# A spectral filter and a gated MLP on one core: early root table, one-tensor small sums, a moved zero fill and another load order of the filter

## The chip, the cores and the metric

The kernel runs on one core of a Trainium2 chip. The metric is the device time of the core in microseconds (us); lower is better.

The engines, as the profile names them: PE is TensorE (matmuls), PEld its weight loads, DVE is VectorE, ACT is ScalarE, POOL is GpSimd, SP is SyncE, which here only issues DMA transfers ("SPq" in a line is its queue).

## The reference, cut to what matters

```python
x = A_x                                               # 1 x 2048 x 576, bf16
X = rfft2(layernorm(x)); X = X * (w_r + 1j * w_i)     # complex filter, 2048 x 289
h  = x + irfft2(X)
h2 = h + (gelu(LN(h) @ w_gate) * (LN(h) @ w_up)) @ w_down   # 576 -> 4608 -> 576
```

The transform is done as matmuls with tables. The MLP is about 430 us of dense matmuls. Before it come three stages that this study is about:

- **Stage A**, layer norm and the first transform. x comes in 16 tiles (0 to 15). For each tile, VectorE or ScalarE takes the sums, then a root on ScalarE, a reciprocal on VectorE, a scaling of the table ATB into ATS, and matmuls.
- **Stage F**, the filter, 16 groups. Each group has a matmul step D, a step B, a product T with the filter (VectorE), sums Z and ZR (VectorE), a step V, and for every four groups a step R. ScalarE moves the results of D (to CUS), B (to YS) and V out of the accumulators, "evictions"; the 16 small pieces of R (to VR) go out on VectorE or ScalarE.
- **The inverse stage**, which needs all of F, and ends with the first gate/up matmul of the MLP.

## The kernel before: the parts that matter

Each engine runs its own queue in the order in which the program lists the operations; the letters in two long strings are that order (cut here).

```python
SEQ1 = "k14 B0 S3 B1 v0 q0 B2 c0 n0 Q3 v1 x0D q1 S5 Q5 c1 x1P M0 ..."   # stage A
SEQF = "D0 D1 D2 B0 B1 T0 T1 D3 D4 B2 Z1 Z0 B3 T2 T3 D5 ..."            # stage F
RENG = [[dve,dve,act,dve],[dve,dve,dve,act],[act,dve,dve,dve],[dve,act,dve],[dve]]  # who evicts R

# SP issues, in this order: x tiles and tables, then 36 small transfers of the filter
for f in w_loads(1, 0, SP) + w_loads(0, 0, SP) + w_loads(0, 1, SP) + w_loads(1, 1, SP): f()
#        imaginary half 1    real half 1          real half 2          imaginary half 2
P.op(POOL, memset(VR, 0.0), w=["Vz"])                 # zero fill, at the start

# small sums of a tile whose statistics ScalarE took: two SBUF tensors each
P.op(DVE, scalar_tensor_tensor(TM, SA0, 1/(D*D), SA0, mult, mult))
P.op(DVE, scalar_tensor_tensor(MV, SA1, 1/D, TM, mult, subtract))

for i in range(16):                                   # "flips": minus the imaginary plane
    P.op(POOL, tensor_scalar(WS[:, g, 0], WS[:, g, 2], -1.0, ...),
         r=[imaginary half of g, ("ATS", 15)], w=[("Wn", i)])
# T(i):  TP = YS * WS     waits for YS(i), both planes of its half, and flip i
# VR evictions wait for the zero fill ("Vz")
```

Of the kernel before, what the change touches and what calls it, by code (L numbers as in the profile page):

```python
# [6 lines left out]
ACTF = mybir.ActivationFunctionType  # L7
ALU = mybir.AluOpType

S, D, K2 = 2048, 576, 289  # L10
KW = 288
HK = 144
NZ = 5
ABASE = 1
FF = 4608
NT = 16
# [3 lines left out]
EPS = 1e-5  # L20
NPRE = 8
GROUPS = ((0, 2), (2, 4), (4, 7), (7, 10), (10, 13), (13, 16))
SEQ1 = """k14 B0 S3 B1 v0 q0 B2 c0 n0 Q3 v1 x0D q1 S5 Q5 c1 x1P M0 B4 E1A B6 v2 E2A E3D n1 B7 q2 E4A n2 c2 B11 B8 E0A Q9 S9 x2P k104 M1 E5A E9A v3 B10 E6A B12 q3 c3 v4 E7A E8A x3D n3 S14 k202 M2 E11A n4 E14D E10A q4 Q14 E12A c4 B13 B15 v5 E13A M3 x4P E15A E16A q5 E18A E17D M4 E19A c5 x5D E20A E21D E22D n5 M5 E23A E25A E26A E27A E24D E28D E29A""".split()
ACT_TILES = tuple(int(w[1:]) for w in SEQ1 if w[0] == "Q")
SEQF = """D0 D1 D2 B0 B1 T0 T1 D3 D4 B2 Z1 Z0 B3 T2 T3 D5 D6 V1 Z2 B4 Z3 D7 V0 B5 T4 Z4 T5 D8 B6 R0 Z5 B7 D9 V3 T6 T7 B8 D10 Z6 B9 T8 V2 V4 D11 Z7 R1 Z8 B10 D12 T9 T10 V5 Z9 Z10 B11 V8 D13 B12 T11 V6 V7 Z11 D14 T12 R2 B13 Z12 D15 B14 T13 V11 Z13 B15 T14 V9 V12 Z14 V10 T15b T15a V14 V13 Z15b Z15a R4 V15 R3""".split()
RENG = [['dve', 'dve', 'act', 'dve'], ['dve', 'dve', 'dve', 'act'], ['act', 'dve', 'dve', 'dve'], ['dve', 'act', 'dve'], ['dve']]
QR = ((0, 2), (2, 4), (4, NPRE), (NPRE, 16))
SEQ = """I0 I1 N0 I2 s0 N1 I3 N2 m0 s1 I4 r0 q0 s2 N3 c0 m1 s3 n1 n0 r1 I5 q1 N4 I6 A1 c1 n3 A0 n2 N5 I7 D2 z3 N6 N7""".split()

# [277 lines left out]
def _build(nc, A_x, A_w_r, A_w_i, B_w_gate, B_w_up, B_w_down, out):  # L307
    P = Prog(nc)
    T = build_tables()
    dram = {n: nc.inline_tensor(_np_bf16(T[n]), name="c_" + n.lower()) for n in T}  # L310
    PE, DVE, ACT, SP, POOL = "pe", "dve", "act", "sp", "pool"
# [16 lines left out]
    VR = sb.alloc("VR", [128, NT, 2, NG, 8], BF16)  # L328
# [18 lines left out]
    MV1 = sb.alloc("MV1", [128, NT, 2], F32)  # L347
    SA = sb.alloc("SA", [128, 2, NT], F32)
    RS1 = sb.alloc("RS1", [128, NT], F32)
    SB2 = sb.alloc("SB2", [128, 2, NT], F32)  # L350
    TM = sb.alloc("TM", [128, 2, NT], F32)
    RS2 = sb.alloc("RS2", [128, NT], F32)
    EPT = sb.alloc("EPT", [128, 1], F32)
# [29 lines left out]
    TP = sb.alloc("TP", [128, 2, 2, 2, KW], BF16)  # L383
    ZS = sb.alloc("ZS", [128, NZ, 2, 256], BF16)
    ZR = sb.alloc("ZR", [128, 2, 2, 128], BF16)
# [14 lines left out]
        return PS[:, b * 512:(b + n) * 512].rearrange("p (a c) -> p a c", a=n)[:, :, 0:w]  # L400


    P.op(POOL, lambda g: g.memset(ZD[:, :], 0.0), w=["ZD"])
    P.op(POOL, lambda g: g.memset(EPT[:, :], EPS), w=["EPT"])
    xv = A_x[0].rearrange("(p c) d -> p c d", c=NT)
    ov = out[0].rearrange("(p c) d -> p c d", c=NT)
    tabs = dram["ATAB"].rearrange("p (c k) -> p c k", c=NT)
# [19 lines left out]
    def w_loads(pl, hf, eng):  # L427
        g0, g1 = ((1, 9), (9, 16))[hf]
        src = (A_w_r, A_w_i)[pl]
        o = []  # L430
        for jj in range(4):
            o.append((WS[jj:64:4, g0:g1, 1 + pl, :], 1 + (16 * jj + g0) * K2, [[128 * K2, 16], [K2, g1 - g0], [1, K2 - 1]], jj))
            o.append((WS[64 + jj:128:4, g0:g1, 1 + pl, :], 1 + (64 + 16 * jj + 16 - g0) * K2, [[128 * K2, 16], [-K2, g1 - g0], [1, K2 - 1]], 4 + jj))
        if hf:
            for p0 in range(2):
                o.append((WS[64 * p0:64 * p0 + 64, 0, 1 + pl, :], 1 + 64 * p0 * K2, [[128 * K2, 16], [16 * K2, 4], [1, K2 - 1]], 8 + p0))
        return [lambda d=d, off=off, ap=ap, h=h: P.dma(eng, d, bass.AP(src.tensor, off, ap), f"w{pl}{hf}", w=[("W", hf, pl, h)]) for d, off, ap, h in o]

    for f in w_loads(1, 0, SP) + w_loads(0, 0, SP) + w_loads(0, 1, SP) + w_loads(1, 1, SP):
        f()  # L440
    GORD = list(range(1, NG)) + [0]
    wkeys = [[("W", hf, pl, h) for pl in range(2) for h in range(8 + 2 * hf)] for hf in range(2)]
# [4 lines left out]
    P.dma(SP, IDT[:, :], dram["EYE"][:, :], "eye", w=["IDT"])  # L447

    P.op(POOL, lambda g: g.memset(U[64:128, 4, :, :, :], 0.0), w=["Uz"])
    P.op(POOL, lambda g: g.memset(VR[:, :, :, :, :], 0.0), w=["Vz"])  # L450



# [12 lines left out]
    def ln1_var(i):  # L466
        c0, c1 = GROUPS[i]
        for c in range(c0, c1):
            if c in ACT_TILES:
                P.op(DVE, lambda v, c=c: v.scalar_tensor_tensor(TM[:, 0, c:c + 1], SA[:, 0, c:c + 1], 1.0 / (D * D), SA[:, 0, c:c + 1],  # L470
                                                                op0=ALU.mult, op1=ALU.mult), r=[("SA0", c)], w=[("TM", c)])
            else:
                P.op(DVE, lambda v, c=c: v.bn_aggr(MV1[:, c, :], ST1[:, c, :, :]), r=[("ST1", c, 0), ("ST1", c, 1)], w=[("MV1", c)])
        for c in range(c0, c1):
            if c in ACT_TILES:
                P.op(DVE, lambda v, c=c: v.scalar_tensor_tensor(MV1[:, c, 1:2], SA[:, 1, c:c + 1], 1.0 / D, TM[:, 0, c:c + 1],
                                                                op0=ALU.mult, op1=ALU.subtract), r=[("SA1", c), ("TM", c)], w=[("MV1", c)])

    def ln1_sqrt(i):
        c0, c1 = GROUPS[i]  # L480
# [20 lines left out]
    def a_bank(i, k):  # L501
        return (5 * i + AORD.index(k) + ABASE) % 8

# [34 lines left out]

    ENG = {"A": ACT, "D": DVE, "P": POOL}
    RUN1 = {"k": idle_mm, "S": act_sum, "Q": act_sq, "B": ln1_tile, "v": ln1_var, "q": ln1_sqrt, "c": ln1_rs, "M": a_mm, "x": ln1_scale, "E": a_ev, "n": x_neg}  # L540
    for w in SEQ1:
        a = w[1:]
        RUN1[w[0]](*((int(a[:-1]), ENG[a[-1]]) if a[-1] in ENG else (int(a),)))

# [6 lines left out]
    FB, used = {}, [0] * 8  # L551
    for t, w in enumerate(SEQF):
        k, i = w[0], w[1:].rstrip("abc")
        if k in "DB":
            late = ("V", 0) in FB or any(x[0] == "V" for x in SEQF[t:t + 4])
            b = min((0, 2, 4) if late else (0, 2, 4, 6), key=lambda b: max(used[b], used[b + 1]))
# [23 lines left out]
    def st_B(i, eng=ACT):  # L580
        sl, s3, sp_ = i % 2, i % 3, 1 if GORD[i] == 0 else 0
        b0 = FB["B", i]
        for b, tabs in ((b0, (0, 1)), (b0 + 1, (1, 2))):
            for m, tb in enumerate(tabs):
                P.op(PE, lambda t, b=b, tb=tb, m=m, s3=s3, sp_=sp_: t.matmul(bank(b, 0, 128, 0, KW), BT[:, sp_, tb, :], CUS[:, s3, m, :], start=(m == 0), stop=(m == 1)),  # L585
                     r=[("CU", s3), "BT"], w=[("PS", b)])
        ev(eng, YS[:, sl, :, :], banks(b0, 2, KW), [("PS", b0), ("PS", b0 + 1)], [("Y", sl)])
# [10 lines left out]
    def st_Z(i, hs=(0, 1)):  # L598
        sl, z3 = i % 2, i % NZ
        if 0 in hs:  # L600
            P.op(DVE, lambda v: v.tensor_tensor(ZS[:, z3, :, :], TP[:, sl, :, 0, 0:256], TP[:, sl, :, 1, 0:256], op=ALU.add), r=[("T", sl, 0)], w=[("Z", z3)])  # L601
        if 1 in hs:
            q, j = (i // 4 % 2, i % 4) if i < LAST else (0, 0)
            P.op(DVE, lambda v: v.tensor_tensor(ZR[:, q, :, 32 * j:32 * j + 32], TP[:, sl, :, 0, 256:KW], TP[:, sl, :, 1, 256:KW], op=ALU.add),  # L604
                 r=[("T", sl, 1)], w=[("ZR", q, j)])

    def st_V(i, b=6, eng=ACT):
        g, z3, sp_ = GORD[i], i % NZ, 1 if GORD[i] == 0 else 0
        for c in range(2):
            for zp in range(2):  # L610
                P.op(PE, lambda t, b=b, c=c, zp=zp, sp_=sp_, z3=z3: t.matmul(bank(b, 0, 128, 256 * c, 256 * c + 256), ZS[:, z3, zp, c:256:2], VT[:, sp_, zp, :],  # L611
                                                                            start=(zp == 0), stop=(zp == 1)), r=[("Z", z3), "VT"], w=[("PS", b)])
        for k0, k1, e in ((0, 4, eng),) if eng is not None else ((0, 2, ACT), (2, 4, ACT)):
            ev(e, V[:, :, k0:k1, g, :].rearrange("p n k e -> p k n e"), bank(b, 0, 128, 128 * k0, 128 * k1).rearrange("p (k n e) -> p k n e", k=k1 - k0, n=16),
               [("PS", b)], [("V", g, k) for k in range(k0 // 2, k1 // 2)])
# [16 lines left out]
    for i in range(NG):  # L632
        P.op(POOL, lambda v, g=GORD[i]: v.tensor_scalar(WS[:, g, 0, :], WS[:, g, 2, :], -1.0, 1.0, op0=ALU.mult, op1=ALU.mult),
             r=[k for k in wkeys[0 if 1 <= GORD[i] < 9 else 1] if k[2] == 1] + [("ATS", NT - 1)], w=[("Wn", i)])
    for w in SEQF:
        i = int(w[1:].rstrip("abc"))
        if w[0] == "D":
            st_D(i)
        elif w[0] == "B":
            st_B(i)  # L640
        elif w[0] == "T":
            if w[-1] in "ab":
                st_T(i, *((0, 256, (0,)) if w[-1] == "a" else (256, KW, (1,))))
            else:
                st_T(i)
        elif w[0] == "Z":
            st_Z(i, {"a": (0,), "b": (1,)}.get(w[-1], (0, 1)))
        elif w[0] == "V":
            st_V(i, FB["V", i], ACT if i < LAST else None)
        elif w[0] == "R":  # L650
            st_R(i, RENG[i], FB["R", i])

# [294 lines left out]
```

## Time and profile before

497.08 us, median of 4 runs (496.99 to 497.31).

The head of the page of before, and its largest group (columns of the group: line, engine, operation, tiles, shapes, count, then busy us and mean ns of one, then idle us of the engine before it):

```profile
span 495.3 us, 9884 instructions
## 1 busy us (share of the span) xinstructions
PE 484.7 (98%) x4338; PEld 288.4 (58%) x4338; DVE 193.7 (39%) x417; ACT 161.3 (33%) x304; POOL 35.2 (7%) x52
...
L823 PE MATMUL PS<-HT,WG 64*128 64x512 bf16 x2106 | 228.5, 376 | 0.0
```

And the chain of waits of before, where the inverse stage (L683) and the MLP (L823) begin (start, length, what; "issue" is time in which nothing was waited for that the profile shows):

```profile
52.75 1.70 PE PS L683 x12
...
65.18 70.11 PE PS L823 x648
```

From 65.18 us on, TensorE never waits. A change before that point can only move the start of this line; everything after it follows rigidly. What sets the 65 us differs by stage.

The places that the change aims at. First the table loads of ScalarE (timeline of before: start, length, engine, line, operation, out<-in, count; in brackets, the idle time before it and what ended it):

```profile
0.74 1.28 ACT L455 ACT_TABLE_LOAD   x1 [0.74 <-PEq L932]
...
5.26 1.28 ACT L481 ACT_TABLE_LOAD   x1
6.55 0.29 ACT L481 ACTIVATE RS<-MV,EPT 128x2 f32<-128x2 f32 x1
```

Then two of the small sums on VectorE (timeline of before), and the Pool instructions at the same moments:

```profile
9.70 0.10 DVE L470 SCALAR_TENSOR_TENSOR TM<-SA 128x1 f32<-128x1 f32 x1
...
9.91 0.86 DVE L476 SCALAR_TENSOR_TENSOR MV<-SA,TM 128x1 f32<-128x1 f32 x1
```

```profile
9.85 0.91 POOL L536 TENSOR_SCALAR XN<-XO 128x864 bf16<-128x864 bf16 x1 [0.15 <-POOL XN L536]
```

The sum at 9.91 works on one element per partition and takes 0.86 us; it ends at 10.77, when the Pool instruction ends (10.76). Those that are not held take 0.10 to 0.17.

Last the filter: what SP issues (timeline of before), and the waits around it (engine and line, what released it, us in total, times, longest):

```profile
6.63 5.33 SPq L217 DMA_DIRECT2D WS<-in_A_w_i_dram  x8
12.00 12.02 SPq L217 DMA_DIRECT2D WS<-in_A_w_r_dram  x18
24.05 6.94 SPq L217 DMA_DIRECT2D WS<-in_A_w_i_dram  x10
```

```profile
POOL WS L633 <- DMA WS<-in_A_w_i_dram: 8.2, 1, 8.2
DVE TP L595 <- ACT YS L566: 4.4, 3, 3.5
...
PE PS L621 <- DVE ZR L604: 1.4, 1, 1.4
```

The second eight flips wait 8.2 us for the imaginary plane's second half and then run from 32.6 to 38.0, in the middle of VectorE's products. The first product T starts at 25.75, when its YS is evicted (timelines of before, Pool's and then VectorE's):

```profile
32.60 5.44 POOL L633 TENSOR_SCALAR WS<-WS 128x288 bf16<-128x288 bf16 x8 [8.21 <-DMA WS<-in_A_w_i_dram]
```

```profile
25.75 1.43 DVE L595 TENSOR_TENSOR TP<-YS,WS 128x1152 bf16<-128x1152 bf16 x2 [3.53 <-ACT YS L566]
```

### The profile page before, as it was taken

Reading aid. Unit: us, or ns where it says so; the run is one execution under the profiler, and the core shown is the slowest. Engines: PE = TensorE matmul, PEld = TensorE weight load, DVE = VectorE, ACT = ScalarE, POOL = GpSimd, SP = SyncE. Lnnn points to the kernel's source line nnn. Section 1 sums busy time; section 2 is a strip of 40 time slices with the busy share of each in tenths; the row PEclk is TensorE's granted clock in tenths of the full one; section 3 lists DMA queues with packets and bytes.
Section 4 is the critical chain, followed back from the end, with each engine's and each line's share of the span. In section 5 each row is a group of like instructions: output and inputs, shape, how many; then the busy total and the mean of one; then the engine's idle time right before and its main releaser. Section 6 shows DMA issues by size and latency. Waiting matters only on the chain.

```text
span 495.3 us, 9884 instructions
## 1 busy us (share of the span) xinstructions
PE 484.7 (98%) x4338; PEld 288.4 (58%) x4338; DVE 193.7 (39%) x417; ACT 161.3 (33%) x304; POOL 35.2 (7%) x52
## 2 busy tenths in 40 slices
PE   6898999999999999999999999999999999999998
PEld 3686655555588854444477744444677544444775
DVE  6789753444365543433311144433211233333111
ACT  6999865233312243233300033233100133233000
POOL 7631701000000010000000000000000000000000
PEclk9999999999999999999999999999999999999999
DMA  7665798511000062000000001000000000000000
GB/s 282 166 184 210 263 346 280 191 25 24 6 13 13 19 195 56 19 9 1 1 13 19 19 14 23 20 1 1 7 17 14 14 1 1 1 1 2 12 19 19
DMA packets 27164, 31.26 MB, mean 63 GB/s; under 512 B 11664, under 2 KB 20112, under 8 KB 27120
## 3 DMA queue, kind: packets, MB, share of 16 engines
q1 hardware_dynamic: 24224, 18.68, 12.9%
q0 software_dynamic: 2896, 11.95, 7.1%
q8 instruction: 34, 0.56, 0.5%
q14 instruction: 10, 0.08, 0.1%
HBM read 26.28 MB, written 2.36 MB: 58 GB/s over the span
## 4 chain that ended last, share of the span: by engine, by line
PE 88%; DVE 2%; issue 0%; ACT 0%; DVEq 0%
PE PS L823 57%; PE PS L873 29%; PE PS L840 1%; PE PS L683 1%; PE PS L722 1%; DVE TP L595 1%; DVE XO L725 0%; PE PS L854 0%; PE PS L611 0%; DVE ZS L601 0%; DVE VR L566 0%; DVE HN L756 0%; PE PS L776 0%; DVE ZR L604 0%; DVE TM L733 0%
## 5 line engine op out<-in xcount | busy, mean ns | idle before, releaser
L823 PE MATMUL PS<-HT,WG 64*128 64x512 bf16 x2106 | 228.5, 376 | 0.0
L823 PEld LDWEIGHTS PS<-HT,WG 64*128 64x128 bf16 x2106 | 107.3, 94 | 119.8 <-issue 1.0
L832 ACT ACTIVATE GL<-PS 128x512 bf16<-128x512 f32 x144 | 85.9, 597 | 257.3 <-PE PS L823 245.0
L833 DVE TENSOR_TENSOR AT<-GL,PS 128x512 bf16<-128x512 bf16 x144 | 98.9, 687 | 175.0 <-ACT GL L832 175.0
L873 PE MATMUL PS<-WD,AT 128*128 128x288 bf16 (+2 forms) x1152 | 144.2, 286 | 0.0
L873 PEld LDWEIGHTS PS<-WD,AT 128*128 128x128 bf16 x1152 | 110.8, 98 | 30.7 <-ACT GL L832 1.3
L876 DVE TENSOR_TENSOR OS<-PS,XO 128x288 bf16<-128x288 f32 (+2 forms) x32 | 14.6, 457 | 100.3 <-PE PS L873 100.3
L823 PE MATMUL PS<-HT,WGX 64*128 64x512 bf16 x486 | 53.4, 376 | 0.0
L823 PEld LDWEIGHTS PS<-HT,WGX 64*128 64x128 bf16 x486 | 23.7, 94 | 28.8
L713 ACT ACTIVATE JD<-XO 128x576 bf16<-128x576 bf16 x8 | 5.5, 683 | 28.5 <-DVE XO L857 28.5
L522 PE MATMUL PS<-ATS,XO 128*128 128x128 bf16 (+1 forms) x128 | 10.5, 221 | 4.3 <-DVE ATS L496 1.9
L595 DVE TENSOR_TENSOR TP<-YS,WS 128x1152 bf16<-128x1152 bf16 (+2 forms) x17 | 12.1, 736 | 4.7 <-ACT YS L566 4.4
L575 PE MATMUL PS<-FT,U 128*128 128x288 bf16 x96 | 13.9, 286 | 0.0
L566 ACT ACTIVATE CUS<-PS 128x576 bf16<-128x576 f32 x16 | 12.9, 834 | 0.5 <-PE PS L575 0.4
L522 PEld LDWEIGHTS PS<-ATS,XO 128*128 128x128 bf16 (+1 forms) x128 | 7.5, 97 | 7.3 <-DVE ATS L496 2.7
L575 PEld LDWEIGHTS PS<-FT,U 128*128 128x128 bf16 x96 | 9.1, 98 | 2.6 <-ACT U L531 0.3
L464 DVE BATCH_NORM_STATS2 ST<-XO 128x6 f32<-128x288 bf16 x24 | 9.2, 439 | 3.7 <-DMA XO<-in_A_x_dram 3.7
L566 ACT ACTIVATE YS<-PS 128x576 bf16<-128x576 f32 x16 | 10.3, 658 | 0.3 <-DVE TP L595 0.2
L585 PE MATMUL PS<-CUS,BT 128*128 128x288 bf16 x64 | 10.1, 286 | 0.0
L756 DVE TENSOR_SCALAR HN<-XO,TM,RS 128x576 bf16<-128x576 bf16 (+1 forms) x32 | 10.0, 362 | 0.0
L857 DVE SCALAR_TENSOR_TENSOR XO<-PS,XO 128x576 bf16<-128x576 f32 x8 | 6.1, 757 | 8.0 <-PE PS L854 8.0
L566 ACT ACTIVATE V<-PS 128x512 bf16<-128x512 f32 (+1 forms) x17 | 9.1, 584 | 0.2 <-PE PS L611 0.2
(77 smaller groups left out, 220.7 us busy)
## 6 DMA issues: line engine op xcount, KB each, us to landing
WD<-in_B_w_down_dram POOLq DMA_DIRECT2D x9, 576.0 KB, 21.7
WG<-in_B_w_up_dram SPq DMA_DIRECT2D x4, 1152.0 KB, 6.5
WG<-in_B_w_gate_dram POOLq DMA_DIRECT2D x4, 1152.0 KB, 9.8
out_dram<-OS SPq DMA_DIRECT2D x30, 72.0 KB, 1.6
XO<-in_A_x_dram SPq DMA_DIRECT2D x3, 576.0 KB, 7.1
WGX<-in_B_w_gate_dram POOLq DMA_DIRECT2D x1, 1152.0 KB, 6.6
WGX<-in_B_w_up_dram SPq DMA_DIRECT2D x1, 1152.0 KB, 10.2
HT<-HN SPq DMA_TRANSPOSE x60, 2.4
```

The lines of the kernel that those rows point to most:

```text
L464: P.op(DVE, lambda v, c=c, h=h: v.bn_stats(ST1[:, c, h, :], XO[:, c, 288 * h:288 * h + 288]), r=[("X", c)], w=[("ST1", c, h)])
L522: P.op(PE, lambda t, b=b, lhs=lhs, p0=p0, p1=p1, s=s, e=e, o=o, c=c: t.matmul(bank(b, p0, p1, o, o + 128), lhs, ATS[:, c, :], start=s, sto ...
L566: fn = (lambda v: v.tensor_copy(dst, src)) if eng == DVE else (lambda a: a.activation(dst, src, ACTF.Copy))
L575: P.op(PE, lambda t, b=b, m=m, us=us, o=o, g=g: t.matmul(bank(b, 0, 128, 0, 2 * HK), U[:, us, g, :, :], FT[:, 3 * o + (2 if us == 4 else u ...
L585: P.op(PE, lambda t, b=b, tb=tb, m=m, s3=s3, sp_=sp_: t.matmul(bank(b, 0, 128, 0, KW), BT[:, sp_, tb, :], CUS[:, s3, m, :], start=(m == 0) ...
L595: P.op(DVE, lambda v: v.tensor_tensor(TP[:, sl, :, :, q0:q1], y4, w4, op=ALU.mult), r=[("Y", sl), ("Wn", i)] + wkeys[0 if 1 <= g < 9 else ...
L756: P.op(eng, lambda v, c=c, hs=hs, o0=o0, o1=o1, x0=x0, x1=x1: v.tensor_scalar(HN[:, hs, o0:o1], XO[:, c, x0:x1], TM[:, 1, c:c + 1], RS2[:, ...
L823: op = P.op(PE, lambda t, h0=h0, kt=kt, wt=wt, b=b, s=(not second and j == 0), e=(second and j == n - 1): t.matmul(bank(b), wg_tile(slot)[ ...
L832: P.op(ACT, lambda a: a.activation(GL[:, s2, :], bank(b0), ACTF.Gelu_apprx_tanh), r=[("PS", b0)], w=[("GL", s2)])
L833: P.op(DVE, lambda v: v.tensor_tensor(AT[:, f, :], GL[:, s2, :], bank(b0 + 1), op=ALU.mult), r=[("GL", s2), ("PS", b0 + 1)], w=[("AT", f)])
L873: P.op(PE, lambda t, b=b, d0=d0, d1=d1, f=f, p=p: t.matmul(bank(b, 0, 128, 0, d1 - d0), AT[:, f, 128 * p:128 * p + 128], WD[:, f, d0:d1], ...
L876: P.op(DVE, lambda v, b=b, d0=d0, d1=d1, p=p, c=c: v.tensor_tensor(OS[:, p % 2, d0:d1], bank(b, 0, 128, 0, d1 - d0), XO[:, c, d0:d1], op=A ...
```

## The change

Its intent: load the root table while the first x transfer is under way; make the small sums operations with one SBUF tensor, so that Pool can't hold them; bring the imaginary plane in first, so that all flips run in one go before the products begin; move the zero fill behind them, so that Pool is free in stage A. Both order strings were rearranged to fit, and three of four R evictions on ScalarE went to VectorE.

```diff
-SEQ1 = """k14 B0 S3 B1 v0 q0 B2 c0 n0 Q3 v1 x0D q1 ...      # strings cut
+SEQ1 = """k14 B0 B1 v0 Q2 S2 B3 q0 v1 n0 n2 c0 q1 S4 x0D ...
-SEQF = """D0 D1 D2 B0 B1 T0 T1 D3 D4 B2 ...
-RENG = [['dve', 'dve', 'act', 'dve'], ['dve', 'dve', 'dve', 'act'], ['act', 'dve', 'dve', 'dve'], ['dve', 'act', 'dve'], ['dve']]
+SEQF = """D0 D1 B0 D2 D3 T0 B1 D4 T1 B2 ...
+RENG = [['dve', 'dve', 'dve', 'dve'], ['dve', 'dve', 'dve', 'dve'], ['dve', 'dve', 'dve', 'act'], ['dve', 'dve', 'dve'], ['dve']]
-    for f in w_loads(1, 0, SP) + w_loads(0, 0, SP) + w_loads(0, 1, SP) + w_loads(1, 1, SP):
+    for f in w_loads(1, 0, SP) + w_loads(1, 1, SP) + w_loads(0, 0, SP) + w_loads(0, 1, SP):
-    P.op(POOL, lambda g: g.memset(VR[:, :, :, :, :], 0.0), w=["Vz"])
-    ... v.scalar_tensor_tensor(TM[..c], SA[:, 0, c], 1.0 / (D * D), SA[:, 0, c], op0=mult, op1=mult)
+    ... v.tensor_scalar(TM[..c], SA[:, 0, c], SA[:, 0, c], 1.0 / (D * D), op0=mult, op1=mult)
-    ... v.scalar_tensor_tensor(MV1[..c], SA[:, 1, c], 1.0 / D, TM[..c], op0=mult, op1=subtract)
+    ... v.tensor_scalar(MV1[..c], SA[:, 1, c], 1.0 / D, TM[..c], op0=mult, op1=subtract)
+    P.op(ACT, lambda a: a.activation(SA[:, 0, 0:1], EPT[:, 0:1], ACTF.Sqrt), r=["EPT"], w=[("SA0", 0)])
     for i in range(NG):
         P.op(POOL, ... flip i ...)
+        if i == NVZ:                                   # NVZ = 15: behind all 16 flips
+            P.op(POOL, lambda g: g.memset(VR[:, :, :, :, :], 0.0), w=["Vz"])
```
(Also, the small constant EPT is filled before ZD.)

More of the change, by code (lines that the diff above doesn't have):

```diff
@@ L13 @@
 NZ = 5
+NVZ = 15
 ABASE = 1
@@ L22 @@
 GROUPS = ((0, 2), (2, 4), (4, 7), (7, 10), (10, 13), (13, 16))
-SEQ1 = """k14 B0 S3 B1 v0 q0 B2 c0 n0 Q3 v1 x0D q1 S5 Q5 c1 x1P M0 B4 E1A B6 v2 E2A E3D n1 B7 q2 E4A n2 c2 B11 B8 E0A Q9 S9 x2P k104 M1 E5A E9A v3 B10 E6A B12 q3 c3 v4 E7A E8A x3D n3 S14 k202 M2 E11A n4 E14D E10A q4 Q14 E12A c4 B13 B15 v5 E13A M3 x4P E15A E16A q5 E18A E17D M4 E19A c5 x5D E20A E21D E22D n5 M5 E23A E25A E26A E27A E24D E28D E29A""".split()
+SEQ1 = """k14 B0 B1 v0 Q2 S2 B3 q0 v1 n0 n2 c0 q1 S4 x0D c1 M0 E1A B6 E0A Q4 B5 B7 x1P v2 E2D n1 B8 E3A E4A k104 M1 q2 c2 B9 Q10 E5A E7A n3 v3 S10 B12 E6A q3 c3 x2P B11 k202 M2 E9A x3P Q13 v4 E12A E8A q4 n4 B14 c4 B15 E10A E11A S13 E13D M3 E14A E15A v5 x4P E16D q5 E17A c5 E18A M4 n5 x5D E20D E19A E22D E21A M5 E23D E24A E25A E27A E26D E29A E28D""".split()
 ACT_TILES = tuple(int(w[1:]) for w in SEQ1 if w[0] == "Q")
-SEQF = """D0 D1 D2 B0 B1 T0 T1 D3 D4 B2 Z1 Z0 B3 T2 T3 D5 D6 V1 Z2 B4 Z3 D7 V0 B5 T4 Z4 T5 D8 B6 R0 Z5 B7 D9 V3 T6 T7 B8 D10 Z6 B9 T8 V2 V4 D11 Z7 R1 Z8 B10 D12 T9 T10 V5 Z9 Z10 B11 V8 D13 B12 T11 V6 V7 Z11 D14 T12 R2 B13 Z12 D15 B14 T13 V11 Z13 B15 T14 V9 V12 Z14 V10 T15b T15a V14 V13 Z15b Z15a R4 V15 R3""".split()
-RENG = [['dve', 'dve', 'act', 'dve'], ['dve', 'dve', 'dve', 'act'], ['act', 'dve', 'dve', 'dve'], ['dve', 'act', 'dve'], ['dve']]
+SEQF = """D0 D1 B0 D2 D3 T0 B1 D4 T1 B2 Z0 Z1 D5 T2 Z2 B3 D6 T3 B4 T4 D7 B5 Z4 D8 Z3 V0 B6 T5 Z5 T6 V1 B7 V3 Z6 T7 D9 R0 B8 D10 V2 Z7 D11 T8 B9 V6 B10 Z8 T9 R1 B11 V4 Z9 D12 D13 V5 T10 B12 T11 Z10 V7 B13 Z11 T12 T13 D14 R2 V9 D15 B14 V8 B15 Z12 V10 Z13 V13 V11 T14 Z14 V12 V14 T15a T15b Z15b Z15a R3 V15 R4""".split()
+RENG = [['dve', 'dve', 'dve', 'dve'], ['dve', 'dve', 'dve', 'dve'], ['dve', 'dve', 'dve', 'act'], ['dve', 'dve', 'dve'], ['dve']]
 QR = ((0, 2), (2, 4), (4, NPRE), (NPRE, 16))
@@ L400, in banks @@
         return PS[:, b * 512:(b + n) * 512].rearrange("p (a c) -> p a c", a=n)[:, :, 0:w]
+    P.op(POOL, lambda g: g.memset(EPT[:, :], EPS), w=["EPT"])
     P.op(POOL, lambda g: g.memset(ZD[:, :], 0.0), w=["ZD"])
-    P.op(POOL, lambda g: g.memset(EPT[:, :], EPS), w=["EPT"])
     xv = A_x[0].rearrange("(p c) d -> p c d", c=NT)
@@ L469, in ln1_var @@
             if c in ACT_TILES:
-                P.op(DVE, lambda v, c=c: v.scalar_tensor_tensor(TM[:, 0, c:c + 1], SA[:, 0, c:c + 1], 1.0 / (D * D), SA[:, 0, c:c + 1],
-                                                                op0=ALU.mult, op1=ALU.mult), r=[("SA0", c)], w=[("TM", c)])
+                P.op(DVE, lambda v, c=c: v.tensor_scalar(TM[:, 0, c:c + 1], SA[:, 0, c:c + 1], SA[:, 0, c:c + 1], 1.0 / (D * D), op0=ALU.mult, op1=ALU.mult), r=[("SA0", c)], w=[("TM", c)])
             else:
@@ L475, in ln1_var @@
             if c in ACT_TILES:
-                P.op(DVE, lambda v, c=c: v.scalar_tensor_tensor(MV1[:, c, 1:2], SA[:, 1, c:c + 1], 1.0 / D, TM[:, 0, c:c + 1],
-                                                                op0=ALU.mult, op1=ALU.subtract), r=[("SA1", c), ("TM", c)], w=[("MV1", c)])
+                P.op(DVE, lambda v, c=c: v.tensor_scalar(MV1[:, c, 1:2], SA[:, 1, c:c + 1], 1.0 / D, TM[:, 0, c:c + 1], op0=ALU.mult, op1=ALU.subtract), r=[("SA1", c), ("TM", c)], w=[("MV1", c)])
     def ln1_sqrt(i):
```

## The prediction

> **What bounds the kernel.** By the per-engine timeline, the first gate/up matmul starts at 65.18 us; from there to the end (493) TensorE has no gap (idle before that group: 0.0). The change touches nothing there, so only the first 65 us (13% of the span) can move: stage A (layer norm and first transform, 0 to 22 us), the filter stage F (22 to 52.7), and the inverse stage (52.75 to 65.18, untouched, starts when F ends).
>
> **Stage A.** VectorE is busy 9.93 of the 10 us from 10 to 20; it sets the pace.
> - Root table: ScalarE loads a table at 0.74 and again at 5.26 (1.28 us each); the first root runs at 6.55, though its sums were ready at 5.53. The second load goes away (the Trainium skill, "ScalarE: Activation LUTs", section "What ACT_TABLE_LOAD costs", has 1283 ns; the trace agrees). Two statistics passes now go ahead of the root, so the first reciprocal comes at about 6.2 to 6.8 instead of 6.88, the first real matmul about 0.7 us earlier than 7.94.
> - Small sums: three of eight two-tensor sums took 0.86, 0.46 and 0.46 us instead of 0.10 to 0.17, each ending with the Pool instruction beside it (10.77 with 10.76, 18.81 with 18.80). That is the lock in the Trainium skill, "SBUF — State Buffer", section "Who interferes with whom": VectorE with two SBUF inputs against Pool reads. One-tensor sums save about 1.4 us.
> - One 3-tile scaling (0.4 us) goes from VectorE to Pool.
> After the 7.85 us landing of x tiles 4 to 7, VectorE needed 12.0 us to its last scaling; now about 10.2. Stage A ends about 2 us earlier, near 20.
>
> **Stage F keeps only part of it.** The first filter product (25.75) needs the real plane's first half. SP issues 36 filter transfers, one per 0.667 us, from 6.63 to 31.0. Now that half is issued in places 19 to 26, the last at 23.4, landing about 2.3 later: 25.7. So VectorE cannot start F earlier than before, whatever A saves; I expect a new wait of some 4 to 5 us there on that DMA. ScalarE and TensorE run ahead (five D, two B evictions), which CUS and YS buffers limit, then stall 1 to 2 us.
> In return: three VR evictions leave ScalarE (about 0.25 each), which is 9.7 of 10 busy from 20 to 50 (0.66 + 0.52 + 0.47 = 1.65 us per group; TensorE about 1.7). The sign flips no longer wait 8.2 us for the imaginary plane: all 16 run back to back, about 18.3 to 26.5, where VectorE is nearly idle; before, eight of them at 32.6 to 38.0 stretched VectorE by about 0.9 us and ended in a 1.4 us TensorE gap (38.2 to 39.6). The moved zero fill (3.5 us) then runs at 26.5 to 30: it only writes, so by the same skill section it should not block VectorE; the trace has no such overlap. VR's first eviction is at 33 or later.
> From 25.7, VectorE has 22.4 us of work to the last Z, plus 0.5 contention; with 1.5 to 2 us of bubbles and the tail, F ends near 51.3 instead of 52.75.
>
> **Prediction:** 495.6 us, 80% range 494.3 to 496.9. Faster by over 2%: 0.005; within: 0.99; slower: 0.005.
>
> **What would show it:** one table load before 2.5 us; no small sum over 0.25; last scaling near 18; first product near 25.7 after a DMA wait; flips done by 27; the first gate/up matmul near 63.7, the rest shifted rigidly.
>
> **What would break it:** the fill blocking VectorE (up to 3.5 us later, slower than before); faster SP issue (first product at 24, another us gained); TensorE cooling in its new gap; the new order causing more bubbles.

## More of the kernel before

Busy time of each engine in two stretches of stage F, before (start:end, length, then busy us and instruction count of each engine, clock, DMA share, GB/s):

```profile
20.00:28.00 8.00, 8.00 (x80) 6.17 (x81) 4.39 (x12) 7.61 (x16) 3.44 (x8) 1.00 0.41 94
28.00:52.00 24.00, 22.28 (x184) 17.33 (x183) 21.75 (x55) 23.42 (x43) 6.97 (x11) 1.00 0.58 191
```

From 28 to 52 us ScalarE (fourth engine figure) is busy 23.42 of 24 us, VectorE 21.75: ScalarE and TensorE pace the filter, VectorE has some slack.

## The result, and the profile after

496.55 us, median of 4 runs (496.37 to 496.71): 0.53 us less than before by the medians. The ratio is 0.9989, with a 95% interval of 0.9971 to 1.0006. Ratios in this text are the mean time of one kernel's fast runs over the mean of the other's in the same rounds, so they are not quite the ratio of the medians quoted. The predicted time was 495.6 with a range of 494.3 to 496.9: the range holds, the change is "within 2%" as forecast, but the gain is about a third of the 1.5 us expected.

The chain of waits after, at the start of the inverse stage and of the MLP; the MLP starts 0.41 us earlier than before:

```profile
52.44 1.63 PE PS L684 x12
...
64.77 70.11 PE PS L824 x648
```

ScalarE's table load, and a small sum with the Pool instruction inside which it runs (timelines of after): one load only, and no sum over 0.21 us.

```profile
0.74 1.28 ACT L539 ACT_TABLE_LOAD   x1 [0.74 <-PEq L933]
```

```profile
16.84 0.16 DVE L475 TENSOR_SCALAR MV<-SA,TM 128x1 f32<-128x1 f32 x1
```

```profile
16.55 0.91 POOL L534 TENSOR_SCALAR XN<-XO 128x864 bf16<-128x864 bf16 x1
```

So stage A became faster as meant: VectorE's last scaling, which started at 19.65 before, starts at 17.67, 2.0 us earlier. What VectorE does next (timeline of after, VectorE):

```profile
17.67 0.58 DVE L494 TENSOR_SCALAR ATS<-ATB,RS 128x128 bf16<-128x128 bf16 x3
18.16 2.40 DVE L529 CAST U<-PS 128x384 bf16<-128x384 f32 x5
27.26 1.43 DVE L594 TENSOR_TENSOR TP<-YS,WS 128x1152 bf16<-128x1152 bf16 x2 [6.70 <-DMA WS<-in_A_w_r_dram]
```

The first product starts at 27.26, which is 1.5 us *later* than before, and it waits 6.7 us for the real plane. The reason is in what SP issues (timeline of after); what Pool does with it stands in the fence behind (Pool's timeline):

```profile
6.76 12.71 SPq L218 DMA_DIRECT2D WS<-in_A_w_i_dram  x18
19.51 12.57 SPq L218 DMA_DIRECT2D WS<-in_A_w_r_dram  x18
```

```profile
18.39 4.02 POOL L632 TENSOR_SCALAR WS<-WS 128x288 bf16<-128x288 bf16 x8 [0.93 <-DVE ATS L494]
22.57 4.02 POOL L632 TENSOR_SCALAR WS<-WS 128x288 bf16<-128x288 bf16 x8 [0.15 <-POOL WS L632]
26.65 3.52 POOL L635 MEMSET VR<- 128x4096 bf16 x1
```

All flips now run back to back and end at 26.6, and the fill runs from 26.65. But the real plane's first half is issued behind 18 imaginary transfers. Its eighth and last transfer is issued at 24.00 and lands 3.2 us later.

All of VectorE's waits in stage F after, 20 to 52 us, and those of before:

```profile
DVE TP L594 <- DMA WS<-in_A_w_r_dram: 6.7, 1, 6.7
```

```profile
DVE TP L595 <- ACT YS L566: 4.4, 3, 3.5
DVE VR L566 <- PE PS L621: 0.7, 2, 0.6
DVE TP L595 <- DVE ZR L604: 0.2, 1, 0.2
```

After its transfer wait, VectorE has none left: it works through its queue from 27.26 to the end of F. The stretches after, in the columns of the two lines of before:

```profile
20.00:28.00 8.00, 7.57 (x61) 5.38 (x58) 1.30 (x4) 5.52 (x9) 6.88 (x14) 1.00 0.43 93
28.00:52.00 24.00, 21.89 (x176) 16.33 (x176) 23.38 (x62) 23.27 (x42) 4.68 (x5) 1.00 0.62 199
```

From 20 to 28 us VectorE did 1.30 us of work where it did 4.39 before; from 28 to 52 it is busy 23.38 of 24. The first step of the inverse stage starts at 52.44 instead of 52.75. Stage F, counted from its first product, got shorter (25.2 us instead of 27.0), but starts 1.5 us later; the difference is the gain.

### The profile page after: what moved, and what is told of

It reads as the page before. It is cut to its first block, busy times and chain, and to the rows that moved or that the text cites. A ratio compares the mean times of both kernels' runs of the same rounds, so it can differ in the third digit from the quotient of the medians.

```text
span 494.9 us, 9880 instructions
## 1 busy us (share of the span) xinstructions
PE 486.1 (98%) x4338; PEld 288.1 (58%) x4338; DVE 192.4 (39%) x418; ACT 158.9 (32%) x300; POOL 34.6 (7%) x53
## 4 chain that ended last, share of the span: by engine, by line
PE 88%; DVE 4%; issue 1%; ACT 0%; DVEq 0%
PE PS L824 57%; PE PS L874 29%; DVE TP L594 1%; DVE VR L565 1%; PE PS L841 1%; PE PS L684 1%; PE PS L723 1%; DVE ZS L600 1%; DVE XO L726 0%; PE PS L855 0%; DVE ZR L603 0%; PE PS L610 0%; DVE HN L757 0%; PE PS L777 0%; DVE TM L734 0%
## 5 line engine op out<-in xcount | busy, mean ns | idle before, releaser
L565 ACT ACTIVATE YS<-PS 128x576 bf16<-128x576 f32 x16 | 11.3, 705 | 2.3 <-DVE TP L594 2.2
L610 PE MATMUL PS<-VT,ZS 128*128 128x256 bf16 x64 | 9.0, 273 | 1.1 <-DVE VR L565 0.5
```

The source lines that it names most:

```text
L565: fn = (lambda v: v.tensor_copy(dst, src)) if eng == DVE else (lambda a: a.activation(dst, src, ACTF.Copy))
```

## The experiments

Theory W says: in after, a transfer (its place in SP's queue) sets the first product, and VectorE's full queue sets the rest, so that stage A's 2 us fall into the wait. Rivals: (B) ScalarE and TensorE bound F and had run ahead, so the wait is mostly hidden; (S) the new F sequence spoils the gain; (P) stage A's savings pass through but are small.

Twelve kernels ran, five rounds each, all correct. Times are medians with the range of the five runs; before was 497.10 to 497.16.

### 1. Other load orders

**e1_halves**: after, the plane halves interleaved.
```diff
-w_loads(1,0) + w_loads(1,1) + w_loads(0,0) + w_loads(0,1)
+w_loads(1,0) + w_loads(0,0) + w_loads(1,1) + w_loads(0,1)
```

> The kernel after, with one edit: the filter planes are loaded as imaginary half 1, real half 1, imaginary half 2, real half 2 (after has both imaginary halves first). Theory W (the wait for the real plane's first half at 27.26 us holds back stage F): that half lands at about 20.5, the first product starts at about 23.5 when its eviction and sign flip are ready. But the second imaginary half now lands near 26.5, so the second eight flips run at 26.5 to 31 beside VectorE and the zero fill at 31 to 35; the first VR evictions (36.4 in after, some 3.5 us earlier here) wait for the fill. F ends about 51 to 51.5 instead of 52.44: about 495.3 us. Rival B (ScalarE and TensorE bound F, which had run ahead and stalled only 1.8 and 0.9 us there, so the wait is mostly hidden): under 0.5 us gained, 496.2 or more.

Measured: 497.05 us (496.82 to 498.26), slower than after by 0.5: a miss for W (about 495.3), and within rival B's "496.2 or more", but not for B's reason. The first product did start at 23.32, but the second flips, held up to 27.05 by their transfer, took 6.02 us beside VectorE, and the fill behind them ran only from 33.13 to 36.65. Waits of e1, 18 to 53 us:

```profile
PE PS L610 <- DVE VR L565: 2.7, 2, 2.3
...
DVE VR L565 <- POOL VR L635: 1.4, 1, 1.4
```

VectorE's VR eviction waited for the fill, and TensorE behind it for 2.7 us. The load order and the place of the fill belong together: with the fill behind all flips, both imaginary halves have to come first.

**e2_halves_fill7**: e1 with the fill between the two eights of flips.
```diff
-NVZ = 15
+NVZ = 7
```

> As e1_halves, and the zero fill stands between the two eights of sign flips on Pool (after flip 8) instead of behind all 16, so it runs at about 22.4 to 26. Theory W: first product at about 23.5, F takes about 25.2 us from there as in after, plus up to 1 us for the flips that now run beside VectorE and for the smaller head start: F ends at 49 to 50.5, time 493.2 to 494.7 us. Rival B: not under 495.8 us.

Measured: 495.59 us (495.43 to 497.43), ratio to before 0.9975 (0.9961 to 0.9988). That is 0.96 us under after, so the wait was not hidden, but it gives less than W's 1.9 to 3.4. The trace says why. Waits of e2, 18 to 53 us, and three instructions of VectorE's timeline, the first two beside the second flips:

```profile
DVE TP L594 <- issue: 2.9, 1, 2.9
DVE TP L594 <- ACT YS L565: 1.3, 1, 1.3
```

```profile
28.07 0.41 DVE L603 TENSOR_TENSOR ZR<-TP 128x64 bf16<-128x64 bf16 x1
28.39 1.64 DVE L594 TENSOR_TENSOR TP<-YS,WS 128x1152 bf16<-128x1152 bf16 x2
...
33.16 0.18 DVE L603 TENSOR_TENSOR ZR<-TP 128x64 bf16<-128x64 bf16 x1
```

The first product starts 4 us earlier (23.20), the second 2.7 us earlier (25.28 instead of about 27.9; ScalarE evicts two CUS before its YS). From there VectorE has no wait in the list, as in after, but the flips at 27.2 to 33.0 hold it: a ZR takes 0.41 beside a flip and 0.18 without, and added up over this stretch the operations are 1.5 us longer than elsewhere. Of 2.7 us, 1.2 remain at the start of the inverse stage (51.24 instead of 52.44).

**e3_oldorder_fill7**: after with the load order of before, and the fill after flip 8.
```diff
-w_loads(1,0) + w_loads(1,1) + w_loads(0,0) + w_loads(0,1);  NVZ = 15
+w_loads(1,0) + w_loads(0,0) + w_loads(0,1) + w_loads(1,1);  NVZ = 7
```

> The kernel after with the load order of before (imaginary 1, real 1, real 2, imaginary 2) and the zero fill after flip 8. Theory W: first product near 23.5 as in e2, second eight flips at 32.6 to 38 as in before, costing VectorE about 0.9 us there: F ends at 49.5 to 51, 493.7 to 495.2 us, slower than e2 by 0 to 0.8. Rival B: not under 495.8 us.

Measured: 495.37 us (494.92 to 495.58), ratio 0.9962 (0.9948 to 0.9976); just above W's range, and not told apart from e2. All five of its runs lie under all four of after's, and both medians lie under rival B's limit of 495.8.

### 2. Does stage A's saving arrive?

**g1_after_undo_a** and **g2_e3_undo_a**: the root table and the small sums put back as in before, once in after, once in e3.
```diff
-P.op(ACT, activation(SA[:, 0, 0:1], EPT, Sqrt))
-tensor_scalar(TM, ...); tensor_scalar(MV1, ...)
+scalar_tensor_tensor(TM, ...); scalar_tensor_tensor(MV1, ...)
```

> The kernel after without the early root table and with the two-tensor small sums of before: the savings of stage A undone, the load order and all else as in after. Theory W (in after the first product waits for a transfer whose time SP's issue order sets, 27.26 us, and VectorE runs from there to the end of F without a gap): stage A ends 1 to 2 us later, the first product does not move, the time moves by under 0.4 us: 496.3 to 496.95. Rival P (stage A's savings pass through to the end): 1 to 2 us slower than after, 497.5 to 498.5.

> The same undoing in e3_oldorder_fill7, where the first product waits for no transfer. Theory W: here stage A counts, F starts 1 to 2 us later, and the time grows from 495.4 by 0.9 to 2 us: 496.3 to 497.4. If stage A's savings were small in themselves, under 0.4 us: below 495.8.

Measured: g1 496.72 us (496.40 to 496.97), 0.17 over after; g2 496.87 us (496.02 to 497.47), 1.5 over e3. The same two edits are worth 0.17 us where the transfer sets the start of F and 1.5 us where it doesn't. That is what W says and P doesn't, but g1 is no clean test of W. In its trace the last scaling was 1.8 us later than in after (19.43), and the real half landed about 1 us *earlier* (first product at 26.19, after a wait of 3.9 us). F took 26.3 us from there instead of 25.2: the flips, which start after stage A, ended at 29.6 instead of 26.6 and held the first sums. So in g1 the late stage A did cost about 1 us, and an earlier landing gave it back; see section 5. The evidence for W is e2, e3 and g2.

### 3. The F sequence

**e4_old_f**: after with SEQF and RENG of before. **f1_e3_old_f**: e3 with SEQF and RENG of before, which is before plus the stage-A work. (Diff: the two strings of the change put back.)

> The kernel after with the instruction sequence of stage F and the VR eviction engines of before (four pieces on ScalarE instead of one). Theory W: first product still at 27.3; three more VR pieces on ScalarE cost at most 0.75 us and the old order adds bubbles: F ends at 52.4 to 53.4, 496.5 to 497.5 us. Rival S (the new F sequence is what spoils the gain): faster than after by over 0.5 us, under 496 us.

> e3_oldorder_fill7 with the F sequence and VR engines of before: that is before plus the stage-A work alone. Theory W: all of stage F moves earlier by the 2 us that stage A saves (first product 25.75 to about 23.7), so 495.1 us, 494.6 to 495.6. If the new F sequence is worth something by itself when the wait is gone, e3 (495.37) is faster than this.

Measured: e4 497.61 us (496.52 to 497.96; 0.1 above W's range), so the new sequence does not spoil after. It is not shown to be better there either: e4's median is 1.1 us higher, but in its trace the transfer landed 0.8 us later (first product at 28.05), and from the first product F took 25.2 us in both. f1 495.66 us (494.99 to 496.87), ratio 0.9974 (0.9962 to 0.9987). The profiled run of f1 took 494.99 us and shows stage A's saving whole: first product at 23.43 instead of 25.75, inverse stage at 50.67 instead of 52.75. The spread of its five runs, 1.9 us, stayed unexplained, and so e3 and f1 can't be told apart.

**f3_e3_b1_first**: e3 with one pair of evictions swapped, so that the second product starts earlier.
```diff
-D0 D1 B0 D2 D3 T0 B1 D4 T1 B2
+D0 D1 B0 B1 D2 T0 D3 T1 D4 B2
```

> e3_oldorder_fill7 with the second B eviction ahead of the third and fourth D eviction on ScalarE (D0 D1 B0 B1 D2 T0 D3 T1 D4 instead of D0 D1 B0 D2 D3 T0 B1 D4 T1). In e3 VectorE waits for it until 25.48 after its first product at 23.39, and is busy nearly without a gap from there. If VectorE's queue alone sets the end of F, the second product starts about 1.2 us earlier and the time falls by up to 1.2 us, to 494.2 to 494.9. If ScalarE and TensorE set it just as much, it stays within 0.3 us of 495.37.

Measured: 495.46 us (494.98 to 495.91), the same as e3. VectorE did its first two products together at 23.14, then waited 1.2 us for ScalarE at 26.61 and 0.65 us at 29.24. Once the transfer is out of the way, VectorE's queue is not the only limit; ScalarE is as close.

### 4. The load order alone, and the best version

**h1_before_order**: before, with the load order of after and nothing else.
```diff
-w_loads(1,0) + w_loads(0,0) + w_loads(0,1) + w_loads(1,1)
+w_loads(1,0) + w_loads(1,1) + w_loads(0,0) + w_loads(0,1)
```

> The kernel before with one edit: the filter planes in the order of after (both imaginary halves, then both real halves). The zero fill stays at the start. Theory W: the first product, 25.75 us in before and waiting there for its eviction, now waits for the real plane's first half, which landed between 26.2 and 28.1 in the runs that have this order: 0.5 to 2.3 us later. Against that, all flips run before it and the VectorE stretch of 0.9 us and the TensorE gap at 38 go away. Time 496.8 to 498.2 us: the order alone gains nothing. If the flips' collision was the larger item: under 496.5.

Measured: 496.44 us (496.27 to 496.61), ratio 0.9985 (0.9972 to 0.9997). A miss: I expected no gain, and this one line brings about as much as the whole change (0.7 us). Its trace has the transfer wait (4.2 us, first product at 26.46, 0.7 us later than before) and no flips in the middle of F; they run from 20.39 to 29.63, so their end still holds the first sums (a ZR takes 0.41):

```profile
DVE TP L595 <- DMA WS<-in_A_w_r_dram: 4.2, 1, 4.2
...
PE PS L621 <- DVE ZR L604: 0.7, 1, 0.7
```

TensorE's gap of 1.4 us has shrunk to 0.7. In h1 ScalarE was not held up by the later product (busy 5.00 of 5 us from 23 to 28), so here the wait was hidden, as rival B says, and the place of the flips was the larger item. The collision moved to the start of F; it did not vanish.

Two comparisons follow from h1. With this load order, all the rest of the change together brings nothing (496.55 in after, 496.44 in h1). And e4 differs from h1 only by the stage-A work and the moved fill, and is 1.2 us slower: in their traces the last transfer of the real half landed 4.2 us after its issue in e4 and 2.7 in h1, and in e4 ScalarE waited 2.5 us for the product at 28.05. Behind this load order the faster stage A did not help; section 5 has a possible reason.

**h2_e2_old_f**: e2's order and fill with SEQF and RENG of before: the interleaved halves, the faster stage A, the old F sequence.

> e2_halves_fill7 (halves interleaved, fill between the two eights of flips) with the F sequence and VR engines of before; against f1_e3_old_f only the load order differs, so the second eight flips run at about 27 to 33 instead of 33 to 38.4. Theory: the same two-source products of VectorE are stretched, only earlier, where VectorE has more slack in the old sequence, and the TensorE gap at 36 to 38 (1.65 us) shrinks: 494.5 to 495.4 us. If the gap comes from the sequence and not from the flips, the same as f1 (494.99 to 496.87) and the gap stays over 1 us.

Measured: 494.22 us (494.07 to 494.60), ratio to before 0.9942 (0.9928 to 0.9956); below my range, 2.9 us faster than before and 2.3 faster than after. This is the version to keep. Its stretches of F, in the columns used before, and the TensorE gap:

```profile
20.00:28.00 8.00, 8.00 (x67) 6.29 (x67) 4.49 (x10) 7.58 (x13) 6.39 (x7) 1.00 0.36 85
28.00:52.00 24.00, 22.84 (x187) 17.33 (x185) 21.15 (x54) 22.89 (x45) 9.31 (x16) 1.00 0.74 227
```

```profile
PE PS L620 <- DVE ZR L603: 0.4, 1, 0.4
```

TensorE is busy 8.00 of 8 us at the start of F, the gap is 0.4 us instead of 1.65 in f1, and the inverse stage starts at 49.85. The second flips (27.0 to 32.9) meet VectorE where it has slack in the old sequence. Between h2 and e2 only the F strings differ: the *new* sequence, which was no worse than the old one behind the late transfer, is 1.4 us worse without it.

### 5. The two halves of stage A's saving, and a late transfer

**i1_h2_two_tensor** and **i2_h2_no_table**: h2 with the small sums of before; h2 without the early table.

> h2_e2_old_f (494.22 us), where stage A is on the critical path, with the two-tensor small sums of before. In before three of the eight such sums were held by a Pool instruction, 1.4 us of VectorE time in all. If that is worth what I put on it, most of it comes through: 494.8 to 495.6 us. If in the new stage-A sequence no Pool instruction meets them, under 0.3 us: below 494.5.

> h2_e2_old_f without the early root table: ScalarE loads the table again (1.28 us) before the first root. The first real matmul comes up to 1.3 us later, but VectorE waits for the x tiles until 7.98 us anyway, so between 0.2 and 1.0 us should come through: 494.4 to 495.2 us. If ScalarE's lost 1.28 us passes in full: 495.5.

Measured: i1 495.03 us (494.80 to 495.43), 0.8 over h2, as expected; one sum took 0.88 us beside a Pool instruction of 0.92. i2 495.75 us (494.68 to 496.33), 1.5 over h2 by the medians, a miss (I expected 0.2 to 1.0) and more than the table load itself; one of its five runs is only 0.5 over. Its profiled run is the slowest, 496.33 us, and shows one reason: delayed by the load, the first scaling met a Pool instruction (VectorE's timeline, then Pool's). It is not a clean trace: the granted clock was 0.60 from 8 to 12 us (1.00 in h2), and what that cost is not separated.

```profile
7.70 1.15 DVE L494 TENSOR_SCALAR ATS<-ATB,RS 128x128 bf16<-128x128 bf16 x2
```

```profile
7.73 0.91 POOL L534 TENSOR_SCALAR XN<-XO 128x864 bf16<-128x864 bf16 x1 [3.38 <-DMA XO<-in_A_x_dram]
```

In h2 the same two scalings took 0.42 us. The scaling reads one SBUF tensor, so by this one case one tensor alone does not keep an operation clear of Pool; the small f32 sums were never seen held in that form (0.22 us at most in all runs). The table is thus worth about 1.5 us and the sums 0.8, but the two overlap: undone together, in g2, they moved the last scaling by 1.7 us (19.30 instead of 17.60 in e3) and the time by 1.5. The rest of the 2 us by which stage A shrank belongs to its new order and the moved fill, which were not tested alone.

Why the last transfer of the real half took 3.2 us to land in after: SP's timeline just behind its issue, and the DMA view from 24 to 25 us (queue: packets, MB, share; then the issues at 24.00 and at 24.64: count, KB, us to landing):

```profile
24.64 1.67 SPq L218 DMA_DIRECT2D WS<-in_A_w_r_dram  x1
```

```profile
q8 instruction: 1, 0.02, 7.3%
...
WS<-in_A_w_r_dram SPq DMA_DIRECT2D x1, 72.0 KB, 3.2
WS<-in_A_w_r_dram SPq DMA_DIRECT2D x1, 63.0 KB, 3.3
```

A 0.02 MB packet of the instruction queue q8 passes, and the issue beside it takes 1.67 us instead of 0.60. In before, after, e4, h1 and g1 each, two such packets pass while SP issues the filter, and exactly two issues take over 1 us (1.06 to 1.67), beside those packets. In after the other one is the imaginary transfer issued at 16.03 (1.52 us). In the four traces with this load order, the last transfer of the real half was issued between 23.66 and 24.00. The packet passed at 24.7 to 25.4 in after and 25.4 to 26.0 in e4, while that transfer was under way, and it landed 3.2 and 4.2 us after its issue. In h1 the packet passed at 26.0 to 26.6 and in g1 at 26.6 to 27.3, as it had landed or nearly so (2.7 and 2.5 us). That the packet causes the stretched issue or the late landing, and that a faster stage A brings it earlier, is argued from these coincidences and not tested.

## Why the prediction was right or wrong

The range and the class were right. The gain was over-estimated by about a microsecond, and one term holds it. Sums of the prediction against the traces:

| step | predicted | measured |
|---|---|---|
| last scaling of stage A | near 18 | 17.67 to 18.25 |
| first real matmul (7.94 before) | 0.7 earlier | 7.08, 0.86 earlier |
| small sums | none over 0.25 | 0.21 at most |
| flips done | by 27 | 26.6 |
| first product | 25.7 | 27.26 |
| F from first product to its end | 25.6 (51.3 - 25.7) | 25.2 (52.44 - 27.26) |
| first gate/up matmul | 63.7 | 64.77 |

- **The failed step is "that half is issued in places 19 to 26, the last at 23.4, landing about 2.3 later: 25.7. So VectorE cannot start F earlier than before".** The mechanism was right: a new wait on that DMA (6.7 us; I had said 4 to 5), ScalarE and TensorE stalled behind it. The size was off by 1.56 us: the last issue was at 24.00 (0.6 later; one imaginary transfer took 1.52 us to issue, where the longest of the first 26 issues in before took 1.06), and it landed 3.2 us later instead of 2.3. Against it F was 0.4 us shorter than predicted, which leaves the 1.1 us by which the first gate/up matmul missed.
- **"One-tensor sums save about 1.4 us", "the second load goes away".** Right about both, and i1 and i2 confirm that they cost time (0.8 and 1.5 us). The mechanism of the sums is the one that the Trainium skill gives in "SBUF — State Buffer", section "Who interferes with whom": an operation of VectorE with two SBUF inputs contends with a Pool instruction that reads SBUF. And right that stage F "keeps only part of it": in after they bring 0.17 us (g1, with its caution).
- **The zero fill "should not block VectorE".** Right. It ran from 26.65 to 30.17 and the products under it took 0.75 us each, as before it.
- **"In return: three VR evictions leave ScalarE".** Counted as a gain; not a gain in general. With the new sequence (which they belong to) F is as long as with the old one behind the late transfer (25.2 us in after and in e4) and the kernel 1.4 us slower without it (e2 against h2), where VectorE has no wait left in its list. The engines and the order of the strings were not separated.
- **The flips' collision, "stretched VectorE by about 0.9 us and ended in a 1.4 us TensorE gap".** Right, and moving the flips is the part of the change that pays: h1 alone gets 0.7 us, although their end still meets the first products there. My expectation for h1 had weighed it too low.

Where the expected gain went: stage A's 2 us (of which f1 shows all, and g2 1.5 us) fell into the wait for a transfer that the same change had moved behind ten others. h2, which puts those ten after it, gets 2.9 us.

What stays open: why f1 and i2 spread over 1.7 to 1.9 us (the slowest run of six kernels, these two among them, has a granted clock of 0.997, but f1 has a run of 496.55 us at 1.0 too), how much of the new F sequence's loss in e2 is due to the VR engines, and whether the instruction packet delays the transfer.

## What to carry to other kernels

Saving time in a stage pays only if what the next stage waits for comes earlier too; list the next stage's other inputs, and where one is a transfer, its place in the issuing queue is a start time. When two consumers need two planes, load the first half of both before the second half of either, and look at what else (here a fill and the flips on Pool) was placed to suit the old order. A schedule tuned around one late input should be tried again when that input is no longer late.

## What the Trainium skill lacked or had wrong

- "DMA: Bandwidth & Descriptors", section "Anatomy of one DMA — SWDGE (gpsimd) path", calls descriptor generation "small, variable". It describes transfers issued from GpSimd; for an issue from SP the page gives a first-byte latency, but no time in microseconds for which it occupies SP. Here most issues of 36 to 72 KB took 0.60 us, one per 0.64 us, so that 36 of them occupied SP for 24 to 25 us and the issue order decided when stage F started.
- No page that I read says that a packet of the instruction queue can coincide with a stretched SP issue: 1.67 us instead of 0.60 in after, two such issues in each of five traces, and landings of 3.2 and 4.2 us instead of 2.5 in two of them. Only coincidences were seen.
- "SBUF — State Buffer", section "Who interferes with whom", agrees with what was looked at here: two-input sums held by a Pool read (0.86 us instead of 0.10 to 0.17), products not held by a Pool fill (0.75 us). A few two-input sums that start within 0.04 us of a Pool read were not held (0.10 us at 7.07 in before); which of the two came first there is finer than this trace shows. It gives no figure for what a run of Pool reads does to a VectorE at full load: in e2, VectorE lost 1.5 us of a 2.7 us head start in a stretch with eight flips in it, and a 0.18 us sum took 0.41.
